# Earlier token preparation and wider spacing of the weight conversion in a fused attention and MoE kernel

## The chip, the cores and the metric

The kernel runs on one core of one Trainium2 chip. The metric is the device time of one execution in microseconds (us). PE is the matrix engine, DVE, ACT and POOL are the vector, scalar and GpSimd engines, SP is the queue that issues most DMA transfers.

## The reference, cut to what matters

```python
# attention: q, k, v are (4, 8, 576, 64)
q_rot, k_rot = rotate(q), rotate(k)              # RoPE: x1*cos - x2*sin, x1*sin + x2*cos
scores = np.matmul(q_rot, k_rot.transpose(0, 1, 3, 2)) / np.sqrt(D)
attn = np.exp(scores - scores.max(-1, keepdims=True))
attn = attn / (attn.sum(-1, keepdims=True) + 1e-09)
x = np.matmul(attn, v)                           # -> (2304, 512)
# MoE 1: w_in (512, 2048), w_out (2048, 512)
h = np.maximum(x @ w_in, 0.0);  x = h * h @ w_out
# MoE 2: the same sizes, alpha (2048)
h = x @ w_in;  out = (np.maximum(h, 0) + alpha * np.minimum(h, 0)) @ w_out
```

The MoE weights come as float64 and are turned into pairs of float32 numbers on the chip.

## The kernel before

**Attention.** 32 heads are worked in 16 pairs (0 to 15) of 9 steps, 144 steps in all. A step forms scores (L205), takes their maximum (DVE, L208) and exponential (ACT, L209), and for a block of four steps ago transposes (PE, L226), splits into high and low parts (ACT L214 `pth`, DVE L215 `ptl`) and multiplies by v (L271). v is split by POOL (L131, L132, `vs`). Keys and queries of the next pair are rotated and transposed into `nat` (ACT L147, DVE L148), and SP copies them into `kH`, `qT` and `kL` ("the stack" of a pair, L173, twelve DMAs).

**First MoE stage.** Two blocks of 384 tokens ("first blocks") go through layer 1 while its weights are converted: 64 units of 12 matmuls, 32 for `w_in` (L535 to L537, result `ph`) and 32 for `w_out` (L553, result `py`, or `ph` for the second block). A unit is one block by one of 16 weight chunks. After these come all other token blocks and layer 2, from kept weights.

**A weight chunk** is loaded by SP (L379, 512 KB of float64) and goes through C = three DVE operations (L388, L389, L394), "grow" on ACT (L398), S = three DVE operations (L403, L404 and the join's L410), and the join's copy on ACT (L409). Each stage has a distance in units from the chunk's place; a chunk comes every 1.8 units. Beside this, `w_out` units need `gh` (ACT, L490) and `gl` (DVE, L491), and `w_in` units need `g` (ACT L575, then ACT L581 or POOL L583).

**The tokens x of the first blocks** come in eight parts ("x chunks"): SP loads them (L502, L504), POOL adds and scales (L512, L513, `xt`), ACT takes the high part (L520, `xs`) and POOL the low part (L526).

**Order.** The MoE is a generator that attention advances once a step for the last steps; inside a step each job is emitted by its distance, and every engine runs its instructions in the order in which they were emitted. The buffers of q, k, v and RoPE ("front") close when the generator starts, and the MoE takes their place.

Of the kernel before, what the change touches and what calls it, by code (L numbers as in the profile page):

```python
# [10 lines left out]
F32 = mybir.dt.float32  # L11
F32R = mybir.dt.float32r
U32 = mybir.dt.uint32
# [6 lines left out]
B, H, S, D = 4, 8, 576, 64  # L20
HALF = D // 2
NT, DM, DFF = B * S, H * D, 2048
P = 128
# [6 lines left out]
NR = 10  # L30
# [4 lines left out]
KQB, STB, PTB = 2, 2, 3  # L35
RB = 1
ROPE_AT, TURN_AT = 5, (0, 1, 2)
AHEAD_X = 14
OP0, OPD0, OP1, OPD1 = 2, 2, 0, 2
OP, OPD, OV = 0, 2, 3  # L40

# [1 line left out]
def attention(tc, q, k, v, ident, ident_d, rope_d, xd, rd, follow):  # L43
# [10 lines left out]
    with ExitStack() as at:  # L54
        pool = lambda name, bufs, **kw: at.enter_context(tc.tile_pool(name=name, bufs=bufs, **kw))
        front = at.enter_context(ExitStack())
        fpool = lambda name, bufs, **kw: front.enter_context(tc.tile_pool(name=name, bufs=bufs, side="right", **kw))
# [3 lines left out]
        st_ = pool("asums", 1)  # L61
        lds = [fpool("ald0", 1)]
        cp = fpool("acst", 1)
        rp = fpool("arope", 1)
        lds.append(fpool("ald1", 1))
        scored = at.enter_context(ExitStack())
        nat = scored.enter_context(tc.tile_pool(name="anat", bufs=1))
        kq = scored.enter_context(tc.tile_pool(name="akq", bufs=KQB))
        scored.enter_context(tc.manual_schedule(engines={mybir.EngineType.PE}))
# [14 lines left out]
        rot = {}  # L84
# [23 lines left out]
        def rope(n, nm, c0=0, c1=NR, E=G):  # L108
            w = c1 - c0
            x = raw[n // 2 % 2, nm][:, 2 * (n % 2):2 * (n % 2) + 2]  # L110
            x = x.rearrange("p h r (t d) -> p (h r) t d", t=2)[:, c0:c1]
            c, ns, s = ((tabq if nm == "q" else tab)[:, c0:c1, i] for i in range(3))
            if (n, nm) not in rot:
                rot[n, nm] = rp.tile([P, 5, 2, D], F32, name=f"rot{nm}", bufs=2)
            r = rot[n, nm][:, :, c0 // 5:c1 // 5].rearrange("p r j d -> p j r d")
            t1 = rp.tile([P, NR, 2, HALF], F32, name="t1", bufs=RB)[:, 0:w]
            t2 = rp.tile([P, NR, 2, HALF], F32, name="t2", bufs=1)[:, 0:w]
            E.tensor_tensor(out=t1, in0=x, in1=c.unsqueeze(2).to_broadcast([P, w, 2, HALF]), op=ALU.mult)
            E.tensor_tensor(out=t2[:, :, 0], in0=x[:, :, 1], in1=ns, op=ALU.mult)
            E.tensor_tensor(out=t2[:, :, 1], in0=x[:, :, 0], in1=s, op=ALU.mult)  # L120
            t1, t2 = (t.rearrange("p (j r) t d -> p j r (t d)", r=5) for t in (t1, t2))
            E.tensor_tensor(out=r, in0=t1, in1=t2, op=ALU.add)
# [159 lines left out]
        steps = [(n, i, j) for n in range(len(pairs)) for i, j in order]  # L282
        per = len(order)
        load(0, "k", 0, 1, nc.gpsimd)
        table(0)
        load(0, "k", 1, 2, nc.gpsimd)
# [24 lines left out]
        for s in range(len(steps) + LAG + OP + 3 * OPD + 8):  # L311
            if s < len(steps):
                n, i, j = steps[s]
# [12 lines left out]
            if LAG <= s and s - LAG < len(steps):  # L326
                n, i, j = steps[s - LAG]
# [15 lines left out]
            for f, a in later.pop(s, []):  # L343
                f(*a)
            if s == len(steps) - AHEAD_X:
                front.close()
            if s == len(steps) - 1:
                scored.close()
            if s >= len(steps) - AHEAD_X:
                follow()  # L350


NB, W = 6, 384
FIRST = 2
STEPS_AHEAD, EARLY = 8, 2
HELD0, OUT0, OUTX, AHEAD = 4, 7, 2, 2
CONV0, EVERY0, EVERY1, EVERY2 = -8, 1.8, 1.8, 2.9


class Weights:  # L360
# [6 lines left out]

    def __init__(self, tc, mats, pbias, place, done):
        self.nc, self.mats, self.pbias, self.place, self.done = tc.nc, mats, pbias, place, done
        self.parts = {}  # L370

        self.stages = (((-3, self.load), (0, self.convert), (0, self.mask), (1, self.grow), (2, self.sign), (2, self.join)),
                       ((-3, self.load), (0, self.convert), (1, self.mask), (2, self.grow), (3, self.sign), (4, self.join)))

    def load(self, st, *j):
        layer, z, i = j
        src, c = (self.mats[layer][0][:, i * P:(i + 1) * P], KC) if z == 0 else (self.mats[layer][1][i * P:(i + 1) * P, :], 1)
        w64 = st.tile([P, 512, 2], U32, name="w64", bufs=4)
        self.nc.sync.dma_start(out=w64.rearrange("p (c n) t -> p c (n t)", c=c),  # L379
                               in_=src.bitcast(U32).rearrange("(c p) n -> p c n", p=P))  # L380
        self.parts[j] = w64

    def convert(self, st, *j):
        V = self.nc.vector
        w64 = self.parts[j]
        lo, hi = w64[:, :, 0], w64[:, :, 1]
        m = st.tile([P, 512], U32, name="m", bufs=2)
        V.tensor_scalar(m, hi, 0x1FF, None, ALU.bitwise_and)  # L388
        V.scalar_tensor_tensor(out=m.bitcast(F32), in0=lo, scalar=2.0 ** -32, in1=m, op0=ALU.mult, op1=ALU.add)  # L389
        self.parts[j] = lo, hi, m  # L390
# [24 lines left out]
def moe(tc, xd, rd, mats, pbias, dram, al, out):  # L415
# [11 lines left out]
    with ExitStack() as mo:  # L427
        pool = lambda name, bufs, **kw: mo.enter_context(tc.tile_pool(name=name, bufs=bufs, **kw))
# [4 lines left out]
        Xw = [Xf[:, 1024 * k:1024 * k + 1024].rearrange("p (y n) -> p y n", y=2) for k in range(6)]  # L433

        XT = pool("xt", 1, side="right").tile([P, 2, 3, W], F32, name="xt")
        st = pool("st", 1, side="right")
        x2 = dram.tile([P, KC, NT], F32, name="x2")
        XW = FIRST * W

# [4 lines left out]
        at_unit = {u: t for t, u in enumerate(units)}  # L444
# [18 lines left out]
        weights = Weights(tc, mats, pbias, place, done_with)  # L463
# [137 lines left out]
        NF = at_unit[0, FIRST, 0, 0]  # L601

        jobs = {}

        def job(at, stages, *j):
            for d, stage in stages:
                jobs.setdefault(max(int(at // 1) + d, -STEPS_AHEAD - 1), []).append((-d, stage, j))

        conv = [[(d, lambda *j, f=f: f(st, *j)) for d, f in stages] for stages in weights.stages]
        for k in range(2 * FC):  # L610
            if k < HELD0:
                job(CONV0 + 2 * k, conv[0][1:], 0, 0, k)
                continue
            at = EARLY + EVERY0 * (k - HELD0)
            if k >= FC + OUT0 + OUTX:
                at = max(at, at_unit[0, FIRST - 1, 1, FC // 2 - 1] - 2 + EVERY1 * (k - FC - OUT0 - OUTX))
            job(at, conv[0], 0, k // FC, k % FC)
        for k in range(2 * FC):
            job(NF + EVERY2 * k, conv[1], 1, k // FC, k % FC)
        for c in range(KC):  # L620
            for layer in range(2):
                for b in range(0 if layer else FIRST, NB):
                    before = (layer, b - 1) if b else (layer - 1, NB - 1)
                    job((NF - 16 if before == (0, FIRST - 1) else at_unit[before + (1, 0)]) + 4 * c + 1,
                        ((-2, load_x), (0, join_x), (1, high_x), (2, low_x)), layer, b, c)


        for e in range(AHEAD_X):
            for k in range(FIRST * KC):
                for d, stage in ((0, load_x), (2, join_x), (2, high_x), (2, low_x)):  # L630
                    if 3 * k // 2 + d == e:
                        stage(0, *divmod(k, KC))
            if e % 3 == 1 and e // 3 < HELD0:
                weights.load(st, 0, 0, e // 3)
            yield
        late["held0"] = pool("held0", HELD0, side="right")
        ps_h = pool("ps_h", 4, side="right", space=PSUM)
        mo.enter_context(tc.manual_schedule(engines={ET.PE, ET.DVE, ET.Activation, ET.Pool}))

        unfinished = []  # L640
        for t in range(-STEPS_AHEAD - 1, NU + 1):
# [18 lines left out]
            if 0 <= t < NU:  # L660
                layer, b, z, i = units[t]
# [6 lines left out]
@with_exitstack  # L668
def fused_kernel(ctx: ExitStack, tc: tile.TileContext, q, k, v, w_in1, w_out1, w_in2, w_out2, alpha, ident_d, rope_d, out):
    nc = tc.nc  # L670
    const = ctx.enter_context(tc.tile_pool(name="const", bufs=1))
    dram = ctx.enter_context(tc.tile_pool(name="dram", bufs=1, space=DRAM))
    ident = const.tile([P, P], F32, name="ident")
    al = const.tile([P, FC], F32, name="al")
    pbias = const.tile([P, 1], F32, name="pbias")
    nc.gpsimd.memset(pbias, -float(896 * 2 ** 23))
    xd = dram.tile([2, P, KC, NT], F32, name="x1")
    rd = dram.tile([KC, 2, NT], F32, name="r1")
    rest = moe(tc, xd, rd, ((w_in1, w_out1), (w_in2, w_out2)), pbias, dram, al, out)
# [43 lines left out]
```

## Time and profile before

| | |
|---|---|
| median of three runs | 1176.19 us (1176.02 to 1178.01) |
| the profiled execution | 1178.72 us |
| its span in the profile | 1176.9 us |
| PE busy | 1097.0 us, 93% of the span |
| DVE busy | 693.4 us, 59% |
| ACT busy | 567.4 us, 48% |
| POOL busy | 396.3 us, 34% |

The span starts with the first instruction of the profile and ends with the last. Overlapping instructions of one engine are counted once in its busy time. The share of an engine is a mean over stages of very different kinds; the stage of the 64 units lies between 342.3 and 506.0 us, attention ahead of it.

### The profile page before, as it was taken

What the parts mean: (1) busy time and instruction counts of PE and PEld (TensorE: products, weight loads), DVE (VectorE), ACT (ScalarE), POOL (GpSimd) and SP (SyncE); (2) the same over time, 40 slices, a digit from 0 to 9 for tenths busy, and PEclk for the clock granted to TensorE, in tenths of its full rate; (3) what the DMA queues carried; (4) which work ended last, traced back from release to release, by engine and by line L of the source; (5) the groups of instructions that cost most, each with busy time, mean ns of one, the idle gap of its engine ahead of it and who ended that gap; (6) DMA issues with size and microseconds to landing.
All of it is one profiled execution on the core that took longest, in us unless ns stands there. A gap on an engine that the chain in (4) does not pass through costs nothing.

```text
span 1176.9 us, 17871 instructions
## 1 busy us (share of the span) xinstructions
PE 1097.0 (93%) x6480; PEld 1041.5 (88%) x6480; DVE 693.4 (59%) x1211; ACT 567.4 (48%) x1228; POOL 396.3 (34%) x372
## 2 busy tenths in 40 slices
PE   2899999999869979899999999999999999999997
PEld 1789898898859869799999999999998989899996
DVE  3788888888778887857868690223232332323231
ACT  1687878878746544455554643323232222323222
POOL 7957566561442230113131221023140504122140
PEclk9899999999888979999999999999999999999999
DMA  8766676454773432455857648840102001010101
GB/s 241 174 180 174 179 203 180 131 152 121 195 222 116 125 109 84 146 177 184 256 172 247 211 155 256 265 158 7 48 1 54 1 27 27 14 41 7 35 1 27
DMA packets 97495, 150.18 MB, mean 128 GB/s; under 512 B 21760, under 2 KB 66432, under 8 KB 97408
## 3 DMA queue, kind: packets, MB, share of 16 engines
q1 hardware_dynamic: 91792, 138.85, 41.3%
q10 hardware_dynamic: 5360, 10.07, 2.3%
q8 instruction: 51, 0.84, 0.3%
q14 instruction: 36, 0.29, 0.1%
q0 software_dynamic: 256, 0.13, 0.0%
HBM read 84.98 MB, written 35.73 MB: 103 GB/s over the span
## 4 chain that ended last, share of the span: by engine, by line
PE 68%; DVE 16%; ACT 4%; DMA 3%; issue 3%; POOL 3%; SPq 1%; ACTq 0%; POOLq 0%
PE py L553 24%; PE ph L535 9%; PE ph L536 9%; PE ph L537 9%; PE acc L271 5%; PE sc L205 5%; PE ps L226 3%; DVE w L403 3%; DVE m L389 2%; DVE w L404 2%; DVE m L388 2%; DVE gl L491 2%; PE ph L553 2%; DVE w L410 1%; DVE nat L148 1%
## 5 line engine op out<-in xcount | busy, mean ns | idle before, releaser
L535 PE MATMUL ph<-xs,w 128*128 128x384 f32 x768 | 258.6, 337 | 5.6 <-ACT g L575 5.6
L536 PE MATMUL ph<-xs,w 128*128 128x384 f32 x768 | 257.8, 336 | 0.0
L537 PE MATMUL ph<-xs,w 128*128 128x384 f32 x768 | 257.7, 336 | 0.0
L491 DVE TENSOR_TENSOR gl<-g,gh 128x384 fp32r<-128x384 f32 x192 | 109.5, 571 | 193.5 <-ACT gh L490 193.4
L579 POOL TENSOR_TENSOR g<-g,xt 128x384 f32<-128x384 f32 x96 | 101.8, 1060 | 295.6 <-DVE xt L578 295.6
L575 ACT ACTIVATE g<-ph 128x384 f32<-128x384 f32 x192 | 93.7, 488 | 194.7 <-PE ph L537 187.2
L490 ACT ACTIVATE gh<-g 128x384 fp32r<-128x384 f32 x192 | 99.8, 521 | 149.5 <-PE py L553 126.6
L553 PE MATMUL py<-w,gh 128*128 128x512 f32 x504 | 155.3, 389 | 0.0
L535 PEld LDWEIGHTS ph<-xs,w 128*128 128x128 f32 x768 | 145.0, 189 | 7.6 <-ACT g L575 7.3
L553 PE MATMUL py<-gh,w 128*128 128x384 f32 x560 | 148.0, 339 | 2.8 <-ACT gh L490 2.8
L536 PEld LDWEIGHTS ph<-xs,w 128*128 128x128 f32 x768 | 145.0, 189 | 0.2
L537 PEld LDWEIGHTS ph<-xs,w 128*128 128x128 f32 x768 | 145.0, 189 | 0.0
L578 DVE TENSOR_SCALAR xt<-ph,al 128x384 f32<-128x384 f32 x96 | 59.3, 617 | 138.8 <-ACT g L575 131.7
L208 DVE TENSOR_REDUCE nm<-sc 128x1 f32<-128x576 f32 x144 | 105.8, 751 | 22.6 <-PE sc L205 21.2
L583 POOL TENSOR_TENSOR g<-g 128x384 f32<-128x384 f32 x48 | 46.2, 962 | 214.7 <-ACT g L575 206.2
L209 ACT ACTIVATE p<-sc,nm 128x576 f32<-128x576 f32 x144 | 106.4, 740 | 24.3 <-DVE nm L208 17.6
L215 DVE TENSOR_TENSOR ptl<-ps,pth 128x512 fp32r<-128x512 f32 (+1 forms) x160 | 99.8, 631 | 21.7 <-ACT pth L214 19.2
L553 PEld LDWEIGHTS py<-w,gh 128*128 128x128 f32 x504 | 94.5, 188 | 19.4
L214 ACT ACTIVATE pth<-ps 128x512 fp32r<-128x512 f32 (+1 forms) x160 | 86.9, 554 | 40.5 <-PE ps L226 39.4
L553 PEld LDWEIGHTS py<-gh,w 128*128 128x128 f32 x560 | 103.3, 191 | 3.5 <-ACT gh L490 3.5
L553 PE MATMUL py<-gl,w 128*128 128x384 f32 x280 | 95.8, 342 | 2.8 <-DVE gl L491 2.6
L553 PE MATMUL py<-w,gl 128*128 128x512 f32 x252 | 98.2, 390 | 0.0
(118 smaller groups left out, 1987.9 us busy)
## 6 DMA issues: line engine op xcount, KB each, us to landing
w<-in_moe_w_in_dram SPq DMA_DIRECT2D x32, 512.0 KB
w<-in_moe_w_out_dram SPq DMA_DIRECT2D x32, 512.0 KB
wk<-xs SPq DMA_DIRECT2D x32, 512.0 KB
w<-wk SPq DMA_DIRECT2D x30, 512.0 KB
xt<-x SPq DMA_DIRECT2D x72, 192.0 KB
kH<-nat SPq DMA_DIRECT2D x64, 144.0 KB
qT<-nat SPq DMA_DIRECT2D x64, 144.0 KB
kL<-nat SPq DMA_DIRECT2D x64, 144.0 KB
```

The costliest lines, as they stand in the source:

```text
L208: V.tensor_reduce(out=nm, in_=sc[:, :, 0:SH], axis=AX.XY, op=ALU.max, negate=True)
L209: A.activation(out=Pt[n, i][:, j * S:(j + 1) * S].rearrange("p (a b) -> p a b", a=2), in_=sc[:, :, 0:SH], func=AF.Exp, bias=nm, accum_out= ...
L214: A.activation(out=sl(hi), in_=src, func=AF.Copy)
L215: V.tensor_tensor(out=sl(lo), in0=src, in1=sl(hi).bitcast(F32), op=ALU.subtract)
L490: A.activation(out=hi, in_=g, func=AF.Copy)
L491: V.tensor_tensor(out=lo, in0=g, in1=hi.bitcast(F32), op=ALU.subtract)
L535: T.matmul(ph[:, :W], lhsT=wh[:, cs], rhs=xh, start=(c == 0), stop=False)
L536: T.matmul(ph[:, :W], lhsT=wh[:, cs], rhs=xl, start=False, stop=False)
L537: T.matmul(ph[:, :W], lhsT=wl[:, cs], rhs=xh, start=False, stop=(c == KC - 1))
L553: T.matmul(acc, lhsT=x, rhs=y, start=(s0 and k == 0), stop=(s1 and k == 2))
L575: A.activation(out=g, in_=ph, func=AF.Relu)
L579: G.tensor_tensor(out=g, in0=g, in1=mn, op=ALU.add)
```

## The change

The rows of the changed kernel carry line numbers that are one higher inside attention and four higher in the MoE (L208 becomes L209, L403 becomes L407).

- The generator starts 21 attention steps ahead of the end of the scores instead of 14; the x chunks are spaced 9/4 steps apart instead of 3/2. For this the front buffers close earlier, and the rotated keys and the second `vraw` buffer move to a pool that lives as long as the scores.
- The stages of the first four weight chunks get a table of times (`FIRST_AT`, counted in units from the first one). The first chunk's C, grow and sign stand beside attention. Chunks 0 and 1 are loaded early, 2 and 3 after the scores' buffers close, and the staging tiles are split over two pools.
- In layer 1, grow moves one unit later and sign and join move one unit later.
- The x jobs of later blocks start one unit earlier, and their ACT and DVE parts keep their place.

```diff
-AHEAD_X = 14
+AHEAD_X = 21
...
-        rp = fpool("arope", 1)
-        lds.append(fpool("ald1", 1))
+        rt = fpool("arope", 1)
         scored = at.enter_context(ExitStack())
+        lds.append(scored.enter_context(tc.tile_pool(name="ald1", bufs=1)))
+        rp = scored.enter_context(tc.tile_pool(name="arot", bufs=2))
...
-CONV0, EVERY0, EVERY1, EVERY2 = -8, 1.8, 1.8, 2.9
+
+FIRST_AT = (-15, -15, -14, -12, -9), (-9, -9, -9, -7, -7), (-5, -5, -5, -4, -4), (-3, -3, -3, -2, -2)
+EVERY0, EVERY1, EVERY2 = 1.8, 1.8, 2.9
...
-        self.stages = (((-3, self.load), (0, self.convert), (0, self.mask), (1, self.grow), (2, self.sign), (2, self.join)),
+        self.stages = (((-3, self.load), (0, self.convert), (0, self.mask), (2, self.grow), (3, self.sign), (3, self.join)),
...
-        w64 = st.tile([P, 512, 2], U32, name="w64", bufs=4)
+        n = next(self.count)
+        w64 = st[n // 2 % 2].tile([P, 512, 2], U32, name="w64", bufs=2)
...
-        m = st.tile([P, 512], U32, name="m", bufs=2)
+        m = st[n % 2].tile([P, 512], U32, name="m")
...
-                job(CONV0 + 2 * k, conv[0][1:], 0, 0, k)
+                for d, (_, stage) in zip(FIRST_AT[k], conv[0][1:]):
+                    if d < -STEPS_AHEAD - 1:
+                        before.setdefault(AHEAD_X + STEPS_AHEAD + 1 + d, []).append((stage, (0, 0, k)))
+                    else:
+                        jobs.setdefault(d, []).append((0, stage, (0, 0, k)))
...
-                    job((NF - 16 if before == (0, FIRST - 1) else at_unit[before + (1, 0)]) + 4 * c + 1,
-                        ((-2, load_x), (0, join_x), (1, high_x), (2, low_x)), layer, b, c)
+                    job((NF - 16 if prior == (0, FIRST - 1) else at_unit[prior + (1, 0)]) + 4 * c,
+                        ((-2, load_x), (0, join_x), (2, high_x), (3, low_x)), layer, b, c)
...
-                    if 3 * k // 2 + d == e:
+                    if 9 * k // 4 + d == e:
                         stage(0, *divmod(k, KC))
-            if e % 3 == 1 and e // 3 < HELD0:
-                weights.load(st, 0, 0, e // 3)
+            if e in (6, 9):
+                weights.load(st, 0, 0, e // 9)
+            for stage, j in before.get(e, []):
+                stage(*j)
             yield
+        st.append(pool("st1", 1, side="right"))
         late["held0"] = pool("held0", HELD0, side="right")
+        for k in range(2, HELD0):
+            weights.load(st, 0, 0, k)
```

DVE, at the start of the stage (chunks 5 and 6 of `w_in`). `m` is the mask tile and `w64` the float64 chunk, each with its number; before:

```order
L388 TENSOR_SCALAR m_4992<-w64_4925 128x512
L389 SCALAR_TENSOR_TENSOR m_4992<-w64_4925,m_4992 128x512
L394 TENSOR_SCALAR w64_4925<-w64_4925 128x512
L403 SCALAR_TENSOR_TENSOR w64_4925<-w64_4925 128x512
L404 TENSOR_SCALAR w64_4925<-w64_4925 128x512
L410 SCALAR_TENSOR_TENSOR w_5032<-m_4992,w64_4925 128x512
L388 TENSOR_SCALAR m_5035<-w64_4969 128x512
L389 SCALAR_TENSOR_TENSOR m_5035<-w64_4969,m_5035 128x512
L394 TENSOR_SCALAR w64_4969<-w64_4969 128x512
```

The same place in the changed kernel:

```order
L392 TENSOR_SCALAR m_4994<-w64_4932 128x512
L393 SCALAR_TENSOR_TENSOR m_4994<-w64_4932,m_4994 128x512
L398 TENSOR_SCALAR w64_4932<-w64_4932 128x512
L407 SCALAR_TENSOR_TENSOR w64_4870<-w64_4870 128x512
L408 TENSOR_SCALAR w64_4870<-w64_4870 128x512
L414 SCALAR_TENSOR_TENSOR w_5015<-m_4950,w64_4870 128x512
L392 TENSOR_SCALAR m_5037<-w64_4970 128x512
L393 SCALAR_TENSOR_TENSOR m_5037<-w64_4970,m_5037 128x512
L398 TENSOR_SCALAR w64_4970<-w64_4970 128x512
L407 SCALAR_TENSOR_TENSOR w64_4932<-w64_4932 128x512
```

C of a chunk was followed at once by S of the same chunk; now C of the next chunk stands between them.

POOL, in the last two pairs of attention (`vs` is v of pairs 13 to 15, `xt` and `xs` the x chunks); before:

```order
L131 CAST vs<-vraw_111 128x10x64
L132 TENSOR_TENSOR vs<-vraw_111,vs 128x10x64
L131 CAST vs<-vraw_114 128x10x64
L132 TENSOR_TENSOR vs<-vraw_114,vs 128x10x64
L131 CAST vs<-vraw_114 128x10x64
L132 TENSOR_TENSOR vs<-vraw_114,vs 128x10x64
L512 TENSOR_TENSOR xt<-xt 128x384
L513 TENSOR_TENSOR xt<-xt 128x384
L526 TENSOR_TENSOR xs<-xt,xs 128x384
```

The same place in the changed kernel:

```order
L132 CAST vs<-vraw_114 128x10x64
L133 TENSOR_TENSOR vs<-vraw_114,vs 128x10x64
L516 TENSOR_TENSOR xt<-xt 128x384
L517 TENSOR_TENSOR xt<-xt 128x384
L530 TENSOR_TENSOR xs<-xt,xs 128x384
L132 CAST vs<-vraw_117 128x10x64
L133 TENSOR_TENSOR vs<-vraw_117,vs 128x10x64
L516 TENSOR_TENSOR xt<-xt 128x384
L517 TENSOR_TENSOR xt<-xt 128x384
L530 TENSOR_TENSOR xs<-xt,xs 128x384
```

One x chunk now stands ahead of v of pair 14; in the rows that follow, three more stand ahead of v of pair 15, and four behind it. All eight stood behind pair 15's before.

SP, around the stack of pair 15 (`xt` the loads of x chunks); before:

```order
L173 DMA kH<-nat 64x576 x4
L173 DMA qT_119<-nat 64x576 x4
L173 DMA kL<-nat 64x576 x4
L502 DMA xt<-x_64 64x2x384
L173 DMA kH<-nat 64x576 x4
L173 DMA qT_120<-nat 64x576 x4
L173 DMA kL<-nat 64x576 x4
L504 DMA xt<-r_65 64x384
```

The same place in the changed kernel:

```order
L174 DMA kL<-nat 64x576 x4
L508 DMA xt<-r_65 64x384
L506 DMA xt<-x_64 64x2x384
L508 DMA xt<-r_65 64x384
L506 DMA xt<-x_64 64x2x384
L508 DMA xt<-r_65 64x384
L506 DMA xt<-x_64 64x2x384
L508 DMA xt<-r_65 64x384 x3
L506 DMA xt<-x_64 64x2x384 x2
L174 DMA kH<-nat 64x576 x4
```

The rest of x chunk 1 and the whole loads of x chunks 2 and 3 stand between the stacks of pairs 14 and 15, where one load stood before.

## Rows read from the trace of the kernel before

**Rows 1.** Windows: from:to, length, busy and (count) by engine, PE clock, DMA share, GB/s.

```profile
250.00:300.00 50.00, 46.24 (x367) 44.42 (x366) 43.58 (x79) 40.66 (x104) 11.52 (x10) 1.00 0.53 139
303.00:324.00 21.00, 17.51 (x119) 16.69 (x118) 13.57 (x25) 13.99 (x36) 14.18 (x14) 0.84 0.68 191
342.30:506.00 163.70, 145.98 (x770) 140.37 (x769) 134.29 (x225) 81.47 (x151) 26.08 (x25) 0.94 0.41 126
506.00:1176.90 670.90, 663.80 (x3554) 627.80 (x3552) 288.58 (x499) 241.81 (x473) 160.68 (x152) 1.00 0.33 102
```

**Rows 2.** Chain of waits: start, us, what; one undisturbed unit of the stage.

```profile
445.27 2.08 PE py L553 x12
```

**Rows 3.** Timeline of PE: start, us, instruction, [idle before, releaser]; the stage's start.

```profile
342.30 0.34 PE L535 MATMUL ph<-xs,w 128*128 128x384 f32 x1
...
354.56 0.69 PE L535 MATMUL ph<-xs,w 128*128 128x384 f32 x1 [3.76 <-ACT g L575]
...
360.16 0.37 PE L537 MATMUL ph<-xs,w 128*128 128x384 f32 x1
```

**Rows 4.** Waits of PE, 342.3 to 506: us in total, times, longest.

```profile
PE ph L553 <- DVE gl L491: 7.3, 5, 4.0
PE ph L535 <- ACT g L575: 5.6, 5, 3.8
PE py L553 <- ACT gh L490: 2.8, 2, 2.4
PE py L553 <- DVE gl L491: 1.7, 2, 1.6
```

**Rows 5.** Waits of DVE, 342.3 to 506.

```profile
DVE gl L491 <- ACT gh L490: 12.2, 15, 1.5
DVE w L403 <- ACT w L398: 10.1, 15, 0.8
```

**Rows 6.** Timeline of DVE in the stage: a `w_in` chunk, then two `w_out` stretches.

```profile
346.04 0.42 DVE L388 TENSOR_SCALAR m<-w 128x512 uint32<-128x512 uint32 x1
...
348.48 0.69 DVE L403 SCALAR_TENSOR_TENSOR w<-w 128x512 uint32<-128x512 uint32 x1 [0.83 <-ACT w L398]
...
350.28 0.42 DVE L388 TENSOR_SCALAR m<-w 128x512 uint32<-128x512 uint32 x1
...
428.78 1.32 DVE L403 SCALAR_TENSOR_TENSOR w<-w 128x512 uint32<-128x512 uint32 x1
...
435.59 0.55 DVE L491 TENSOR_TENSOR gl<-g,gh 128x384 fp32r<-128x384 f32 x1
436.91 0.56 DVE L491 TENSOR_TENSOR gl<-g,gh 128x384 fp32r<-128x384 f32 x1 [0.77 <-ACT gh L490]
437.39 0.68 DVE L403 SCALAR_TENSOR_TENSOR w<-w 128x512 uint32<-128x512 uint32 x1
...
439.18 0.42 DVE L388 TENSOR_SCALAR m<-w 128x512 uint32<-128x512 uint32 x1
...
440.70 0.55 DVE L491 TENSOR_TENSOR gl<-g,gh 128x384 fp32r<-128x384 f32 x1
```

**Rows 7.** Timelines of POOL, ACT and PE around the first x chunks, and the tail.

```profile
306.49 0.99 POOL L513 TENSOR_TENSOR xt<-xt 128x384 f32<-128x384 f32 x1
...
307.51 0.52 ACT L520 ACTIVATE xs<-xt 128x384 fp32r<-128x384 f32 x1 [1.94 <-POOL xt L513]
...
310.11 0.39 PE L244 MATMUL ps<-ident,p 128*64 128x128 f32 x1 [3.26 <-DVE ptl L215]
...
333.36 0.42 PE L244 MATMUL ps<-ident,p 128*64 128x128 f32 x1 [5.15 <-DVE pttl L215]
```

**Rows 8.** Timelines of POOL, SP and PE: v of pair 14, stack and scores of pair 15.

```profile
285.61 1.55 POOL L132 TENSOR_TENSOR vs<-vraw,vs 128x640 fp32r<-128x640 f32 x1
...
290.70 2.54 SPq L173 DMA_DIRECT2D kH<-nat  x4
...
300.49 0.51 PE L205 MATMUL sc<-kH,qT 128*128 128x288 f32 x2
```

More of the change, by code (lines that the diff above doesn't have):

```diff
@@ L113, in rope @@
             if (n, nm) not in rot:
-                rot[n, nm] = rp.tile([P, 5, 2, D], F32, name=f"rot{nm}", bufs=2)
+                rot[n, nm] = rp.tile([P, 5, 2, D], F32, name=f"rot{nm}")
             r = rot[n, nm][:, :, c0 // 5:c1 // 5].rearrange("p r j d -> p j r d")
-            t1 = rp.tile([P, NR, 2, HALF], F32, name="t1", bufs=RB)[:, 0:w]
-            t2 = rp.tile([P, NR, 2, HALF], F32, name="t2", bufs=1)[:, 0:w]
+            t1 = rt.tile([P, NR, 2, HALF], F32, name="t1", bufs=RB)[:, 0:w]
+            t2 = rt.tile([P, NR, 2, HALF], F32, name="t2", bufs=1)[:, 0:w]
             E.tensor_tensor(out=t1, in0=x, in1=c.unsqueeze(2).to_broadcast([P, w, 2, HALF]), op=ALU.mult)
@@ L369, in __init__ @@
         self.nc, self.mats, self.pbias, self.place, self.done = tc.nc, mats, pbias, place, done
-        self.parts = {}
-        self.stages = (((-3, self.load), (0, self.convert), (0, self.mask), (1, self.grow), (2, self.sign), (2, self.join)),
+        self.parts, self.count = {}, itertools.count()
+        self.stages = (((-3, self.load), (0, self.convert), (0, self.mask), (2, self.grow), (3, self.sign), (3, self.join)),
                        ((-3, self.load), (0, self.convert), (1, self.mask), (2, self.grow), (3, self.sign), (4, self.join)))
@@ L377, in load @@
         src, c = (self.mats[layer][0][:, i * P:(i + 1) * P], KC) if z == 0 else (self.mats[layer][1][i * P:(i + 1) * P, :], 1)
-        w64 = st.tile([P, 512, 2], U32, name="w64", bufs=4)
+        n = next(self.count)
+        w64 = st[n // 2 % 2].tile([P, 512, 2], U32, name="w64", bufs=2)
         self.nc.sync.dma_start(out=w64.rearrange("p (c n) t -> p c (n t)", c=c),
                                in_=src.bitcast(U32).rearrange("(c p) n -> p c n", p=P))
-        self.parts[j] = w64
+        self.parts[j] = n, w64
     def convert(self, st, *j):
         V = self.nc.vector
-        w64 = self.parts[j]
+        n, w64 = self.parts[j]
         lo, hi = w64[:, :, 0], w64[:, :, 1]
-        m = st.tile([P, 512], U32, name="m", bufs=2)
+        m = st[n % 2].tile([P, 512], U32, name="m")
         V.tensor_scalar(m, hi, 0x1FF, None, ALU.bitwise_and)
@@ L435, in moe @@
         XT = pool("xt", 1, side="right").tile([P, 2, 3, W], F32, name="xt")
-        st = pool("st", 1, side="right")
+        st = [pool("st0", 1, side="right")]
         x2 = dram.tile([P, KC, NT], F32, name="x2")
@@ L609, in moe @@
         conv = [[(d, lambda *j, f=f: f(st, *j)) for d, f in stages] for stages in weights.stages]
+        before = {}
         for k in range(2 * FC):
             if k < HELD0:
-                job(CONV0 + 2 * k, conv[0][1:], 0, 0, k)
+                for d, (_, stage) in zip(FIRST_AT[k], conv[0][1:]):
[3 more added lines that the diff above has]
+                        jobs.setdefault(d, []).append((0, stage, (0, 0, k)))
                 continue
@@ L622, in moe @@
                 for b in range(0 if layer else FIRST, NB):
-                    before = (layer, b - 1) if b else (layer - 1, NB - 1)
-                    job((NF - 16 if before == (0, FIRST - 1) else at_unit[before + (1, 0)]) + 4 * c + 1,
-                        ((-2, load_x), (0, join_x), (1, high_x), (2, low_x)), layer, b, c)
+                    prior = (layer, b - 1) if b else (layer - 1, NB - 1)
+                    job((NF - 16 if prior == (0, FIRST - 1) else at_unit[prior + (1, 0)]) + 4 * c,
+                        ((-2, load_x), (0, join_x), (2, high_x), (3, low_x)), layer, b, c)
         for e in range(AHEAD_X):
```

## The prediction

> **What bounds the kernel now.** I read the windows by stage first [rows 1]. From 506.00 to the end the matrix engine is busy 663.80 of 670.90 us at a granted clock of 1.00, and between 250 and 300 us, in steady attention, 46.24 of 50. What is left to win lies between: 303 to 324 us (busy 17.51 of 21, clock 0.84) and the stage of 64 units, 342.30 to 506.00 us, busy 145.98 of 163.70 at clock 0.94. The chain of waits gives the price of an undisturbed unit there, 12 matmuls in 2.08 us [rows 2]; 64 such units are 133.1 us, so the stage loses 163.7 - 133.1 = 30.6 us. The waits of the matrix engine name 7.3 + 5.6 + 2.8 + 1.7 = 17.4 us of it [rows 4]; the other 13.2 are mostly matmuls at the lower clock level after such a wait. The timeline shows one: after a wait of 3.76 us the matmuls from 354.56 to 360.16, 17 intervals, take 5.60 us [rows 3], where 17/12 of a unit at full clock would be 2.95 [rows 2]; 2.65 us lost behind a wait of 3.76.
>
> Behind those waits stand the vector and scalar engines with the conversion. A `w_in` chunk goes round in 350.28 - 346.04 = 4.24 us, 0.83 of it waiting for the scalar engine's grow [rows 6]; the matrix engine uses a chunk up in two units, 4.16 us. The wait for grow is 10.1 us over the stage in 15 records [rows 5]. The vector engine is busy 134.29 us of the stage [rows 1], as much as the matrix engine's ideal 133.1: it is the second bound, close below.
>
> **The wider spacing.** With C of the next chunk ahead of S, three vector operations, 1.5 us together, lie between grow's input and its user: C is 440.70 - 439.18 = 1.52 us, S 439.18 - 437.39 = 1.79 [rows 6], and grow's wait was 0.83. So the 0.83 goes, and a `w_in` chunk costs 3.41 us, below 4.16: in the first 32 units the vector engine no longer falls behind. The wait at the fifth unit also goes. Between the last operations of attention and the first `g`, the old vector order holds S of chunk 0 and C and S of chunks 1 to 3, three and a half cycles; the new one holds chunks 2 and 3, two cycles. One and a half cycles of 4.24 are 6.4 us, more than the wait of 3.76 [rows 3]. With it go the 2.65 us at the lower level.
>
> In the `w_out` half the vector engine also makes `gl`, 0.48 us each (436.91 to 437.39 [rows 6]). By the table of times, twelve units in its first part hold 12 `gl`, about 7 S and 5 C: 5.8 + 12.5 + 7.6 = 25.9 us. Two more terms: where POOL runs x joins beside it, S and C took 435.59 - 428.78 = 6.81 instead of 440.70 - 437.39 = 3.31 us [rows 6], 3.5 more, and two waits for `gh` of 0.77 [rows 6], 1.5. In all 30.9 against 12 x 2.08 = 25.0 for the matrix engine, 5.9 over. It starts two units ahead, 2 x 2.08 - 0.48 = 3.7 us of cover, so about 2.2 us of wait are left. A second part of fourteen units (14 `gl`, 7 C, 7 S, and 2.6 us of waits and POOL's presence) comes to 6.7 + 10.6 + 12.5 + 2.6 = 32.4 against 29.1, 3.3 over: hidden by the cover if that has been won back, up to 3.3 if not; I take half, 1.8. Waits in the stage then sum to 4.0, and as 17.4 us of waits brought 13.2 of other loss, 0.76 for each, another 3.0. The stage: 133.1 + 4.0 + 3.0 = 140.1, a gain of 23.6 us. The bounds: all 30.6 (no wait left), and 10.1 (only grow's wait goes and the vector engine sets the pace).
>
> **The earlier x chunks and the first weight chunk.** Now beside attention: for each of four x chunks two POOL joins and a subtraction of about 0.99 and a copy of 0.52 on the scalar engine [rows 7]; C of chunk 0 and the first two operations of its S, about 2.6 us of the vector engine [rows 6], and grow. In steady attention POOL is busy 11.52 of 50 us, the scalar engine 40.66, the vector engine 43.58 [rows 1], so the work fits on average into about 40 us. But it stands in a fixed order: a copy that waits for POOL holds back the exponentials and splits queued behind it, and the matrix engine waits for those. The one case in the trace is the first x chunk: the copy waited 1.94 us for POOL, then the matrix engine 3.26 us for `ptl` [rows 7], and the window around it has clock 0.84, 21 x 0.16 = 3.4 us at most lost to it [rows 1]. So such a place costs up to 3.26 + 3.4 = 6.7 us. With the slack of the averages it costs nothing. I see two tight places. One is SP's queue: the last loads of x chunk 3 wait for x chunk 1's subtraction, and that follows v of pair 14, which ends at 285.61 + 1.55 = 287.16 [rows 8]. Two joins, the copy and the subtraction, 1.98 + 0.52 + 0.99, give 290.65, and two loads at 2.54/4 us of issuing each 291.9: the stack of pair 15, issued from 290.70, comes some 1.2 us later, and its first score stands at 300.49 [rows 8]. Its own slack no row gives; cost 0 to 1.2. The other is the vector engine with chunk 0. I take one half of a place for all, 3.3 us, with bounds 0 and 6.7. The place at 310.11 itself stays, since the fifth x chunk still follows v of pair 15.
>
> What the trace shows of vector and POOL work side by side: S and C took 6.81 us instead of 3.31 where POOL ran x joins [rows 6]. The Trainium skill, "SBUF — State Buffer", section "SBUF: two separate sides", says that these two engines share a port pair as a lock held for a whole instruction, so that the other blocks fully. The stretch agrees. By that rule the five operations of chunk 0 beside attention, each held for one POOL operation of about 1 us, would cost 5 us instead of 3.3, an estimate; the sum would then be 1.7 higher.
>
> **The tail of attention, 324 to 342.** Four x chunks less, but join of chunk 0 and C and S of chunk 1 more, about 0.7 (some two fifths of S) + 3.3 - 1.5 = 2.5 us of the vector engine ahead of its last splits. The matrix engine waits 5.15 us there for `pttl` [rows 7]; the vector work can fall into that or lengthen it. Zero, bounds -2.5 and 2.5.
>
> **Loads, pools and later x jobs.** The first two weight loads wait less than the old ones, being issued far earlier; a chunk's staging tile is held for 3 + 3 units of 1.8 per chunk, 3.3 of 4 tiles, so loads are not held back. After 506.00 the new order of the x jobs moves only work of engines that are not waited for; 7.1 us of that window are all that could move [rows 1]. Zero for both.
>
> **Sum.** 1176.9 - 23.6 + 3.3 = 1156.6 us of span. The profiled execution took 1178.72 us, 1.8 above its span, so 1158.4; the median 1176.19 is 2.5 below that execution, and so the forecast is 1156 us.
>
> **Rivals.**
> - The vector engine sets the stage's pace. For: it is busy 134.29 us there, beside POOL's joins its operations double, and the waits for `gh`, 12.2 us [rows 5], are not touched. Against: it leaves idle time in the first 32 units that it could use. Then only grow's 10.1 us go: 1176.9 - 10.1 + 3.3 - 0.7 = 1169 us. Chance 0.16.
> - The matrix engine waits nowhere in the stage, and attention absorbs everything: 1176.9 - 30.6 - 0.7 = 1146 us. For: average idle time in attention; against: the second half's balance above. Chance 0.14, of which most falls a little short of 1146.
> - Slower: each of the four x chunks beside attention does what the first one does now, a scalar copy that waits for POOL, splits behind it, and a lower clock after: 4 x 6.7 = 26.8 us. It decides from the fourth such place (23.6 / 6.7 = 3.5). 1176.9 - 23.6 + 26.8 - 0.7 = 1179 us. For: rows 7; against: ahead of x chunks 1 to 3 POOL has been idle long enough and their loads are early. Chance 0.04.
> - The change doesn't do what it says: chunks come no earlier, since loads of chunks 2 and 3, now issued only when the scores' buffers close, make the first conversions late, and the two-and-two staging keeps them so. The stage stays at 163.7: 1176.9 + 3.3 - 0.7 = 1179.5 us. Chance 0.02.
>
> **How the numbers follow.** The forecast's own case has 0.62, with 1150 to 1164 from its bounds. A further 0.02 goes to a near balance, the second case with two bad places in attention. The range 1146 to 1168 leaves out about half of the first rival, the slow cases and a little below. A difference of 0.2%, about 2.4 us, is what a measurement of this kernel can tell from no change. Faster: 0.62 + 0.16 + 0.14 = 0.92; same 0.02; slower 0.04 + 0.02 = 0.06.
>
> **What would show it.** In the profile after: L407 with almost no wait for L402; no wait at the fifth unit; the stage within 137 to 145 us; the remaining waits of L557 for `gl` in the `w_out` half; the first of them beside POOL's x joins. In attention a total longer by at most 7 us, with the loss at x chunks 1 to 3 or the first scores of pair 15. The forecast is wrong if the stage gains under 16 us, or if attention with its tail, up to the first unit, moves by more than 7.

## The result, and the profile after

The changed kernel takes 1165.39 us (1165.12 to 1166.19, 4 runs) against 1176.9 for the one before (4 runs): a ratio of 0.9903 with an interval of 0.9886 to 0.992. It is 11.5 us faster, where 20 were forecast; the range holds it, the likeliest case's own range of 1150 to 1164 does not. The two profiled executions lie a little further apart, 1176.9 and 1163.8 us of span, and the rows below are theirs.

The windows after, cut at the same pieces of work (the first unit now stands at 349.21, the first matmul after the 64 units at 494.51 us):

```profile
250.00:300.00 50.00, 43.27 (x324) 40.80 (x325) 42.12 (x78) 36.75 (x94) 21.80 (x20) 0.97 0.67 179
303.00:324.00 21.00, 18.01 (x131) 17.34 (x130) 15.12 (x27) 15.08 (x38) 10.35 (x11) 0.92 0.56 162
349.20:494.50 145.30, 137.63 (x770) 135.71 (x769) 129.17 (x215) 79.66 (x148) 25.51 (x24) 0.98 0.42 127
494.50:1163.80 669.30, 663.16 (x3554) 627.92 (x3552) 286.95 (x499) 242.62 (x473) 160.18 (x152) 1.00 0.33 103
```

Against [rows 1] the stage went from 163.7 to 145.3 us, 18.4 less; the rest from 670.9 to 669.3; and steady attention, 46.24 us of matrix work in 50 before, has 43.27. Up to the first unit the kernel is 6.9 us later, and as this execution ran 0.7 us ahead at 250 us, attention lost 7.6.

The waits of the matrix engine in the stage after, answering to [rows 4], and of the vector engine, to [rows 5]:

```profile
PE ph L557 <- DVE gl L495: 5.6, 4, 2.5
PE py L557 <- DVE gl L495: 1.9, 1, 1.9
PE ph L557 <- ACT gh L494: 0.2, 1, 0.2
```

```profile
DVE gl L495 <- ACT gh L494: 7.3, 6, 1.6
DVE g L599 <- PE py L557: 2.4, 2, 1.9
DVE w L407 <- ACT w L402: 1.5, 2, 0.8
```

The wait for grow fell from 10.1 to 1.5 us and no unit waits for `g` any more. What is left, 7.7 us, is for `gl` and `gh` in the `w_out` half, most of it for `gl`. The vector engine there, and POOL beside it:

```profile
418.31 2.46 DVE L495 TENSOR_TENSOR gl<-g,gh 128x384 fp32r<-128x384 f32 x2
420.69 1.50 DVE L407 SCALAR_TENSOR_TENSOR w<-w 128x512 uint32<-128x512 uint32 x1
...
423.39 1.38 DVE L414 SCALAR_TENSOR_TENSOR w<-m,w 128x512 fp32r<-128x512 f32 x1
...
426.33 0.55 DVE L495 TENSOR_TENSOR gl<-g,gh 128x384 fp32r<-128x384 f32 x1
```

```profile
417.99 1.08 POOL L587 TENSOR_TENSOR g<-g 128x384 f32<-128x384 f32 x1 [0.61 <-ACT g L579]
419.03 1.32 POOL L516 TENSOR_TENSOR xt<-xt 128x384 f32<-128x384 f32 x1
...
423.15 1.07 POOL L517 TENSOR_TENSOR xt<-xt 128x384 f32<-128x384 f32 x1
```

```profile
426.94 0.69 PE L557 MATMUL ph<-gl,w 128*128 128x384 f32 x1 [2.47 <-DVE gl L495]
```

From 418.31 to 426.33 stand two `gl`, an S and a C: 8.0 us, where the undisturbed rows give 2 x 0.48 + 3.31 = 4.3 [rows 6]. The `gl` that ended at 426.9 is the one for which the matrix engine waited 2.47 us. The scalar engine is not what holds the stretch up: its longest waits in the stage are for the vector engine, the 4.3 us one at 422 us, and its wait rows name no POOL operation.

```profile
ACT w L413 <- DVE w L407: 39.3, 24, 4.3
```

The first `gl` of the `w_out` half is done 1.4 us ahead of its unit (413.80 + 0.56 against 415.78):

```profile
413.80 0.56 DVE L495 TENSOR_TENSOR gl<-g,gh 128x384 fp32r<-128x384 f32 x1
...
415.78 0.33 PE L557 MATMUL py<-gh,w 128*128 128x384 f32 x1
```

In attention the first loss is at the first weight chunk. The timelines of four engines around it, where the first column is the start and the last bracket the idle time before:

```profile
266.67 1.55 POOL L133 TENSOR_TENSOR vs<-vraw,vs 128x640 fp32r<-128x640 f32 x1
267.08 1.42 DVE L392 TENSOR_SCALAR m<-w 128x512 uint32<-128x512 uint32 x1 [0.47 <-DMA w<-in_moe_w_in_dram]
...
268.54 0.68 DVE L393 SCALAR_TENSOR_TENSOR m<-w,m 128x512 f32<-128x512 uint32 x1
269.15 0.75 DVE L209 TENSOR_REDUCE nm<-sc 128x1 f32<-128x576 f32 x1
269.81 0.68 DVE L149 TENSOR_TENSOR nat<-ps,nat 128x512 fp32r<-128x512 f32 x1
269.93 0.74 ACT L210 ACTIVATE p<-sc,nm 128x576 f32<-128x576 f32 x1 [1.61 <-DVE nm L209]
...
270.64 0.63 PE L227 MATMUL ps<-ident,p 128*128 128x128 f32 x4 [2.47 <-DVE nat L149]
```

The mask waited 0.47 us for its load, took 1.42 instead of 0.42 [rows 6] and ended at 268.50, just behind POOL's subtraction (268.22). The maximum and `nat` queued behind it, and the matrix engine waited 2.47 us. The Trainium skill, "SBUF — State Buffer", section "SBUF: two separate sides", says that a GpSimd operation and a vector operation that runs in a 2-port mode or has two SBUF inputs take a shared port pair as a lock, and that the other one is fully blocked for the whole instruction. The trace agrees, with 1.42 us against 0.42; no run shows in which mode this mask, which has one input, ran.

The second kind of loss, at x chunk 3:

```profile
299.07 1.01 POOL L517 TENSOR_TENSOR xt<-xt 128x384 f32<-128x384 f32 x1
...
300.11 0.52 ACT L524 ACTIVATE xs<-xt 128x384 fp32r<-128x384 f32 x1 [2.05 <-DMA kH<-nat]
300.66 0.60 ACT L215 ACTIVATE pth<-ps 128x512 fp32r<-128x512 f32 x1
...
301.15 0.73 ACT L210 ACTIVATE p<-sc,nm 128x576 f32<-128x576 f32 x1
...
302.03 0.52 PE L206 MATMUL sc<-kH,qT 128*128 128x288 f32 x2 [1.37 <-ACT p L210]
```

The copy starts when POOL's join ends (299.07 + 1.01 = 300.08; the transfer that the bracket names is not its input), and an exponential behind it makes the scores wait 1.37 us.

### The profile page after: what moved, and what is told of

Same layout as the page of the kernel before. It is cut to its first block, busy times and chain, and to the rows that moved or that the text cites. A ratio compares the mean times of both kernels' runs of the same rounds, so it can differ in the third digit from the quotient of the medians.

```text
span 1163.8 us, 17882 instructions
## 1 busy us (share of the span) xinstructions
PE 1089.9 (94%) x6480; PEld 1037.0 (89%) x6480; DVE 688.3 (59%) x1211; ACT 568.2 (49%) x1228; POOL 394.6 (34%) x372
## 4 chain that ended last, share of the span: by engine, by line
PE 72%; DVE 14%; DMA 4%; POOL 4%; issue 3%; ACT 2%; SPq 1%; POOLq 0%; DVEq 0%; ACTq 0%
PE py L557 28%; PE ph L540 10%; PE ph L541 10%; PE ph L539 10%; PE acc L272 5%; PE sc L206 4%; PE ps L227 3%; PE ph L557 2%; DVE m L393 2%; DVE w L407 2%; DMA kraw<-in_k_dram 2%; DVE w L408 1%; DVE w L414 1%; DVE nat L149 1%; DVE ptl L216 1%
## 5 line engine op out<-in xcount | busy, mean ns | idle before, releaser
L209 DVE TENSOR_REDUCE nm<-sc 128x1 f32<-128x576 f32 x144 | 105.7, 751 | 22.0 <-PE sc L206 20.6
L216 DVE TENSOR_TENSOR ptl<-ps,pth 128x512 fp32r<-128x512 f32 (+1 forms) x160 | 99.8, 631 | 22.8 <-ACT pth L215 20.7
L227 PE MATMUL ps<-ident,p 128*128 128x128 f32 x576 | 89.1, 278 | 12.9 <-DVE nat L149 9.0
```

The costliest lines, as they stand in the source:

```text
L209: V.tensor_reduce(out=nm, in_=sc[:, :, 0:SH], axis=AX.XY, op=ALU.max, negate=True)
L216: V.tensor_tensor(out=sl(lo), in0=src, in1=sl(hi).bitcast(F32), op=ALU.subtract)
L227: T.transpose(u[:, c * P:(c + 1) * P], p[:, (S + 64) * j + c * P:(S + 64) * j + (c + 1) * P], ident)
```

## The experiments

All kernels give the matrix engine the same work in the same order, so the start of one and the same matmul can be compared between profiles. The table says how many us a kernel gained (-) or lost (+) against the kernel before, between five fixed matmuls that start at 266.30, 273.97, 300.35, 342.30 and 506.03 us there. A column is read from one profiled execution of each kernel; the last column is the median of its runs, with the ratio and its interval.

| kernel | first weight chunk, to 273.97 | x chunks, to 300.35 | rest of attention, to 342.30 | 64 units, to 506.03 | median us; ratio |
|---|---|---|---|---|---|
| the change | +3.5 | +3.6 | +0.4 | -18.4 | 1165.39; 0.9903 (0.9886 to 0.992) |
| e1 | 0.0 | 0.0 | +0.4 | -15.6 | 1162.65; 0.9873 (0.986 to 0.9887) |
| e2 | +2.7 | +4.0 | -0.2 | -7.2 | 1177.69; 1.0002 (0.9992 to 1.0011) |
| e3 | +3.5 | +1.2 | -3.8 | -19.8 | 1160.12; 0.9851 (0.9832 to 0.9871) |
| e4 | +3.2 | +3.7 | +0.4 | -25.8 | 1158.22; 0.9834 (0.9817 to 0.985) |
| e5 | 0.0 | +3.6 | +0.6 | -18.5 | 1161.53; 0.9863 (0.9844 to 0.9882) |
| e6 | +2.4 | +1.1 | -0.7 | -19.6 | 1160.47; 0.9851 (0.9834 to 0.9868) |
| e7 | 0.0 | +1.3 | +3.3 | -19.5 | 1161.43; 0.9859 (0.984 to 0.9877) |
| e8 | 0.0 | 0.0 | -5.3 | -13.1 | 1160.23; 0.985 (0.9832 to 0.9867) |
| e9 | +2.8 | +4.0 | -1.3 | -25.3 | 1158.03; 0.9831 (0.9817 to 0.9845) |
| e10 | 0.0 | 0.0 | -4.3 | -20.0 | 1151.65; 0.9775 (0.9762 to 0.9789) |
| e11 | +3.2 | +1.2 | +0.4 | -26.1 | 1156.61; 0.9821 (0.9807 to 0.9834) |

How far single executions scatter can be read from kernels whose attention holds the same instructions in the same order. Those that keep the early weight chunk beside v of pair 13 have +2.4 to +3.5 in the first column; e3, e6 and e11 have -3.8, -0.7 and +0.4 in the third. Smaller differences in those two columns show nothing.

**e1, the distances alone, on the kernel before.**

```diff
-(1, self.grow), (2, self.sign), (2, self.join)),
+(2, self.grow), (3, self.sign), (3, self.join)),
```

> The kernel before with only the distances of layer 1's conversion changed (grow 1 to 2, sign and join 2 to 3). Theory A (the stage's gain comes from the spacing; attention's loss of the changed kernel comes from the early x chunks and weight chunk): attention ends at 342 as before, no wait of L403 for L398, but the wait of about 4 us at the fifth unit stays with some 2.6 us of matmuls at the lower clock; 1164 to 1167 us. Theory B (without the early weight chunk the first units stay late and the spacing gives little): at most 6 us less than before, 1170 us or more.

Measured 1162.65 us, a little below what theory A gave: this one edit is worth no less than the whole change (0.9873 against 0.9903, intervals that just touch). The stage gains 15.6 us alone and attention loses nothing before the tail. The vector engine's wait for grow is 0.2 us in the stage. The wait at the fifth unit is 0.9 us, not 4: the chunks ahead of the first `g` now follow each other in 350.31 - 346.86 = 3.45 us and not in 4.24.

```profile
346.86 0.69 DVE L403 SCALAR_TENSOR_TENSOR w<-w 128x512 uint32<-128x512 uint32 x1
...
350.31 0.69 DVE L403 SCALAR_TENSOR_TENSOR w<-w 128x512 uint32<-128x512 uint32 x1
```

```profile
PE ph L535 <- ACT g L575: 0.9, 1, 0.9
```

**e2, the early chunks alone.** The changed kernel with the old distances, in layer 1's conversion and in the later x jobs.

```diff
-(2, self.grow), (3, self.sign), (3, self.join)),
+(1, self.grow), (2, self.sign), (2, self.join)),
```

> The changed kernel with the old distances (grow 1, sign and join 2, x jobs as before), so only the early x chunks and weight chunks. Theory A: attention 7 us longer as in the changed kernel, the wait at the fifth unit gone (6 us), all other waits of the stage as before: 1175 to 1180 us, no gain. Theory B (the early start is what pays): 1171 us or less.

1177.69 us, no gain: attention loses 6.5 and the stage gains 7.2. The wait at the fifth unit is gone, which with the slower matmuls behind it was 3.76 + 2.65 us [rows 3]. So the early token and weight work, half of the change, brings nothing by itself. The two parts do not add up in the stage either, 15.6 + 7.2 = 22.8 against 18.4: each removes most of the wait at the fifth unit.

**e3, xs on POOL.**

```diff
-            A.activation(out=xh, in_=xin[layer, b, c][0][:, 0], func=AF.Copy)
+            if first(layer, b):
+                G.tensor_copy(out=xh, in_=xin[layer, b, c][0][:, 0])
+            else:
+                A.activation(out=xh, in_=xin[layer, b, c][0][:, 0], func=AF.Copy)
```

> The changed kernel with the high part of the first blocks' x chunks taken by POOL (a copy) instead of ACT, so that no ACT instruction waits for POOL's x joins. Theory A (ACT's copies that wait for POOL hold back the exponentials behind them): the losses of attention at x chunks 1 to 3 (1.7 and 1.65 us) and a part of those at chunks 4 and 5 go, 3 to 5 us: 1160 to 1162.5 us. Theory B (POOL and DVE hold each other up, and the scalar copy does not matter): four to eight more POOL operations beside DVE, 1165 to 1168 us.

1160.12 us: theory A. The loss at the x chunks falls from 3.6 to 1.2 us, and it is as small in e6, e7 and e11, which have the same edit; the 1.2 that stay were not followed up. The rest of attention gains 3.8 here, but not in e6 and e11. At the place shown above the exponential no longer stands behind a copy, and the same scores stand without a wait:

```profile
299.90 0.74 ACT L210 ACTIVATE p<-sc,nm 128x576 f32<-128x576 f32 x1
...
300.78 0.53 PE L206 MATMUL sc<-kH,qT 128*128 128x288 f32 x2
```

**e4, without the joins of the third block.**

```diff
-            if layer == 0:
+            if layer == 0 and b != FIRST:
                 G.tensor_tensor(out=xr[:, 0], in0=xr[:, 0], in1=xr[:, 1], op=ALU.add)
```

> The changed kernel without the two POOL joins of x for the third token block of layer 1 (its x stays unsummed and unscaled), the operations that ran at 419 to 424 and 474 to 487 us. Theory A (beside POOL's joins DVE's conversions take twice as long, and this makes the waits for gl): the 1.3 and 2.5 us waits at 419 and 427 us and the 1.2 and 1.9 us ones at 477 and 481 us go with half of the lower clock behind them, 5 to 8 us less: 1157 to 1160.5 us. Theory B (DVE has too much to do there whatever POOL does): at most 2 us less, 1163.5 us or more.

1158.22 us, 7.2 below the change, all of it in the stage (-25.8 against -18.4): theory A. Eight POOL operations cost 7.4 us of the stage. The first `gl` of the `w_out` half is as early as in the change; what goes are the slow operations behind it.

**e5, a late first weight chunk.** A 128x1 copy from x chunk 3 into the mask tile holds the conversion back to 300 us.

```diff
+        if j == (0, 0, 0):
+            V.tensor_copy(out=m[:, 0:1].bitcast(F32), in_=self.gate.bitcast(F32))
         V.tensor_scalar(m, hi, 0x1FF, None, ALU.bitwise_and)
...
+        weights.gate = X[:, 1, 3, 0:1]
```

> The changed kernel, whose first weight chunk's conversion on DVE waits for the copy of x chunk 3 (a 128x1 copy from it into the mask tile), so that it no longer stands beside v of pair 13 on POOL. Theory A (the 3.5 us lost at 267 us come from the first mask operation, which took 1.42 us instead of 0.42 beside that POOL copy after waiting for its load): attention is 2.5 to 3.5 us shorter, 1161.5 to 1163 us. Theory B (the conversion costs DVE as much wherever it stands, or collides with x chunks there): 1164.5 to 1167 us.

1161.53 us, theory A: the 3.5 us at 267 us are gone and nothing of them comes back. The run takes away two things at once, the mask's 0.47 us wait for its load and the 1.0 us by which POOL lengthened it, and does not tell them apart. With no POOL operation in the way the same mask takes 0.43 us:

```profile
300.15 0.43 DVE L394 TENSOR_SCALAR m<-w 128x512 uint32<-128x512 uint32 x1
```

**e6, the joins in the first half.** On e3, the third block's first two x chunks loaded and joined at units 10 to 16.

```diff
...
+                    if prior == (0, FIRST - 1) and c < 2:
+                        job(12 + 4 * c, ((-2, load_x), (0, join_x)), layer, b, c)
+                        job(at, ((2, high_x), (3, low_x)), layer, b, c)
+                        continue
...
```

> The kernel of e3 (xs on POOL), with the load and the POOL joins of the third block's first two x chunks issued at units 10 to 16 instead of straight behind the last square of the first half, the whole computation kept. Theory A (the joins hurt only where DVE is the bound): the waits for gl at units 33 to 35 go, 5 to 7 us less than e3: 1153 to 1155.5 us. Theory B (the time that they take from DVE comes back wherever they stand): 1158.5 to 1161 us.

1160.47 us: theory A fell. The stage is as in e3 (-19.6 against -19.8). The vector operations beside the joins are as slow in the first half as in the second:

```profile
371.60 1.38 DVE L414 SCALAR_TENSOR_TENSOR w<-m,w 128x512 fp32r<-128x512 f32 x1
373.02 1.12 DVE L392 TENSOR_SCALAR m<-w 128x512 uint32<-128x512 uint32 x1
```

So the vector engine has no slack in the first half that such work could use. That gave a new theory: it works through the stage almost without a pause, and what POOL takes from it anywhere is paid at the end. e9 and e10 test it.

**e7, e6 with the late first chunk of e5.**

> The kernel of e6 with the late first chunk of e5. Theory A (the three losses are apart and add up): e6 less 2 to 3.5 us, 1150 to 1153 us. Theory B (attention gives the 3.5 us back later anyway, as e3 shows where the loss of 3.5 us at 267 shrinks to 0.9 by the first unit): the same as e6 within 1 us.

1161.43 us, like e6, as theory B said, but not for its reason. The loss at 267 us is gone, and the rest of attention is 4.0 us worse than in e6 (+3.3 against -0.7). Most of that stands at one place, and the copy that holds the conversion back makes it: x chunk 3 is later here than in e5, the copy waits 1.89 us for POOL's subtraction and with it every vector operation behind it, the mask then takes 1.01 us, and the matrix engine waits 3.61 us for a `ptl`; before the same matmul it waited 1.05 us in e6.

```profile
308.99 0.15 DVE L393 COPY m<-xs 128x1 f32<-128x1 f32 x1 [1.89 <-POOL xs L536]
309.18 1.01 DVE L394 TENSOR_SCALAR m<-w 128x512 uint32<-128x512 uint32 x1
...
311.60 0.39 PE L245 MATMUL ps<-ident,p 128*64 128x128 f32 x1 [3.61 <-DVE ptl L216]
```

So this run does not test whether the two losses add up; that stays open.

**e8, the distances and xs on POOL, without the early chunks.** The edits of e1 and e3 on the kernel before.

> The kernel of e1 (the kernel before with the new distances alone) with the x chunks' high part on POOL. Theory A (ACT's copies that wait for POOL make the loss at 306 to 316 us of before): attention is 2 to 4 us shorter than in e1, 1158.5 to 1160.5 us, as good as e3, and the early x chunks and weight chunk of the change then buy nothing. Theory B (the early start is needed once ACT is free): 1162 us or more.

1160.23 us, as e3: theory A, and the early x chunks and weight chunk buy nothing. Attention is 5.3 us shorter than before, 4.5 of it between 300 and 319 us, so that the loss around 310 us of [rows 7] was the copy on ACT. The stage starts so early that it waits more at its own beginning (-13.1).

**e9, the squares on ACT, on the change.**

```diff
-                elif i % 2 == 0:
+                elif i % 2 == 0 or first(layer, b):
                     A.activation(out=g, in_=g, func=AF.Square)
```

> The changed kernel with all squares of the first blocks on ACT (16 of 32 ran on POOL). Theory A (DVE sets the stage's pace: from 349 to 430 us it has next to no idle time, and each POOL operation beside it holds it up by some 0.6 us): DVE's work of the first half gets up to 8 us shorter, the waits for gl at 419 and 427 us go or shrink, 4 to 7 us less than the changed kernel, 1158.5 to 1161.5 us. Theory B (ACT, with 8 us more and its copies and grow in one order with the squares, takes DVE's place): within 1.5 us of it, 1164 us or more.

1158.03 us, 7.4 below the change, as theory A said. From about the first unit to 430 us, first the change, then this kernel, where POOL does nothing:

```profile
349.20:430.00 80.80, 76.76 (x433) 75.87 (x432) 76.07 (x120) 50.17 (x93) 21.04 (x20) 0.98 0.41 126
```

```profile
347.00:430.00 83.00, 83.00 (x484) 83.00 (x484) 72.55 (x134) 62.11 (x116) 0.00 (x0) 1.00 0.43 134
```

The vector engine was busy 76.07 of 80.80 us (94%) for 120 operations, 0.63 us each; now 134 operations, not quite the same mix, take 72.55, 0.54 each, and the matrix engine has no idle time. ACT, with 62.11 of 83, has room for the squares.

The 7.4 us are not the squares' alone. With no square ahead of them in POOL's queue, the joins of the third block's first two x chunks ran ahead too: they stand between 331 and 344 us here, before the stage, and not at 419 to 424, and e4 shows that the joins alone are worth as much. What the squares cost by themselves can be read ahead of 412 us, where no such join stands in either kernel. One of the six vector operations of a chunk, first in the change from 349.2 to 412 us, then in e9 from 347 to 410 (count, busy us, mean ns, idle us before):

```profile
L393 DVE SCALAR_TENSOR_TENSOR m<-w,m 128x512 f32<-128x512 uint32 x16 | 13.3, 832 | 0.6
```

```profile
L393 DVE SCALAR_TENSOR_TENSOR m<-w,m 128x512 f32<-128x512 uint32 x17 | 11.8, 692 | 0.6
```

Three others shrink as well, and over 16 chunks the six means differ by 7.1 us, some 0.5 for each of the 14 squares in that window. So the first `gl` of the `w_out` half is done 3.3 us ahead of its unit (411.68 + 0.56 against 415.51), where it was 1.4 in the change:

```profile
411.68 0.56 DVE L495 TENSOR_TENSOR gl<-g,gh 128x384 fp32r<-128x384 f32 x1 [1.10 <-ACT gh L494]
...
415.51 0.33 PE L557 MATMUL py<-gh,w 128*128 128x384 f32 x1
```

**e10 and e11, the squares on ACT, on e8 and on e3.**

> The kernel of e8 (the kernel before with the new distances and xs on POOL) with all squares of the first blocks on ACT. Theory A: as in e9, 4 to 7 us less than e8, 1153.5 to 1156.5 us, the best so far. Theory B: like e8 within 1.5 us.

> The kernel of e3 (the changed kernel with xs on POOL) with all squares of the first blocks on ACT. If the early x chunks and weight chunk of the change are worth something once DVE has room, this is below e10 by more than 1 us, 1151 to 1154 us; if only the distances pay, it is like e10 or above it.

e10 takes 1151.65 us, 8.6 below e8 and the best of all; e11 1156.61. The stage is better with the early chunks (-26.1 against -20.0), but attention is 9.1 us worse (+4.8 in all against -4.3), of which some 4 lie in the column that scatters by as much. So with vector time freed, the early start costs more than it brings: 5.0 us in the medians. e10 also tells more of the squares than e9 does. In it the joins of the first two x chunks stand at 347 to 359 us, inside the first half as in e6; with the squares on POOL that move changed nothing (-19.6 in e6, -19.8 in e3), and with the squares gone as well the stage gains 6.9 (against e8). The two pairs start from different kernels, so this bears the theory out without proving it. e10 still waits 3.7 us for `gl`, and at its start 2.4 us for the first `g` and 1.2 for a join.

```profile
PE ph L538 <- ACT g L578: 2.4, 1, 2.4
PE py L556 <- DVE gl L491: 1.9, 1, 1.9
PE ph L556 <- DVE gl L491: 1.8, 2, 1.2
PE ph L540 <- DVE w L410: 1.2, 1, 1.2
```

## Why the prediction was right in direction and short in size

- **The wider spacing: right.** The wait for grow went (10.1 to 1.5 us), and e1 shows that this edit alone is worth 15.6 us of the stage. The first 32 units no longer wait, as forecast: from 349.2 to 412 us the matrix engine is busy all the time.
- **The wait at the fifth unit: right, for more than one reason.** It went in the change, and in e2 too, where the early chunks alone remove it. But e1, which keeps the late chunks, has only 0.9 us of it: the shorter chunk cycle would nearly do.
- **The `w_out` half: the mechanism right, the size too small.** Forecast were 4.0 us of waits and 3.0 of other loss; measured 7.7, and 145.3 - 133.1 - 7.7 = 4.5. (Half of 3.3 is 1.7 and not 1.8; that slip is worth 0.1 us.) The failed step is the cover of 3.7 us "two units ahead": the first `gl` was done 1.4 us ahead of its unit. With it fails the sentence in the first rival that the vector engine "leaves idle time in the first 32 units": in the change it is busy 94% of the time to 430 us, and comes to the `w_out` half with little to spare. POOL's x joins were priced rightly where they stand (3.5 us then, 3.7 now); its 16 squares in the first half were given no price, though vector operations are longer beside them too. With the squares gone the cover is 3.3 us (e9), close to the forecast's. e4 shows what the joins cost, 7.4 us of the stage, and e6 that moving them inside the stage changes nothing; how the 6.9 us of e9 divide between squares and joins no run shows. The rival of the vector engine's pace had the right cause with too high a price for it: 1169 us.
- **Attention: the failed term.** 3.3 us were forecast, with 6.7 as bound; 7.6 came. By the clock the first unit moved by 6.9 us; counted from 266 us, by 7.6, a little over the 7 that the forecast named as a sign of being wrong. The half place was two things. The first weight chunk costs 3.5 us by itself, where its first operation waited for its load and then stood beside v of pair 13 on POOL (e5). The forecast knew the doubling beside POOL, but had no place for it in the sum. The x chunks cost 3.6 us, and 2.4 of it go when the copy no longer waits on ACT for POOL (e3): the mechanism of the slower rival, with some 0.8 us for each of the three copies that waited and not 6.7. The other 1.2 us stay open.
- **SP's queue: the mechanism right, its price nothing.** The last loads of x chunk 3 went out at 293.76 us, as soon as x chunk 1's subtraction had ended (293.73), and the stack of pair 15 right behind them at 295.11, half a microsecond after the part of `nat` that `kH` reads was ready (294.62). The forecast gave this 0 to 1.2 us. The matrix engine's wait rows of that stretch name no transfer, so it cost nothing that they show.

```profile
292.73 1.00 POOL L530 TENSOR_TENSOR xs<-xt,xs 128x384 fp32r<-128x384 f32 x1 [0.64 <-ACT xs L524]
293.76 1.25 SPq L506 DMA_DIRECT2D xt<-x  x2
294.23 0.39 ACT L148 ACTIVATE nat<-ps 128x256 fp32r<-128x256 f32 x1
295.11 2.47 SPq L174 DMA_DIRECT2D kH<-nat  x4
```

- **The place at 310 us: right that it stays**, partly: the stretch from 300 to 319 us gained 1.5 us in the change, where e3 and e8 gain 4.2 and 4.5.
- **Tail and the later blocks:** +1.9 us between the matmuls at 319.32 and 342.30 in place of 0, and 1.6 us less after the 64 units: the first inside its bounds of 2.5, the second inside the 7.1 that could move.
- **The range of the likeliest case**, 1150 to 1164 us, is not worked out from its bounds, though the text says so: stage and attention at their ends give 1146 to 1173, and 1165.4 lies inside that.

## What to carry to other kernels

In these runs an operation's time on the vector engine is not a constant: ask for every long stretch of it what POOL runs beside it, and count that POOL work against the vector engine too. Here the matrix engine showed the waits of a stage whose pace a vector engine busy 94% of the time set; moving POOL's work earlier inside that stage gave nothing, and taking it out of the stage or to an engine with room did. Try each half of a change by itself: here one half did it all. When early work is put into a stage that is full, look at what stands behind each of its instructions in the same queue, above all behind a copy that waits for a third engine. And when an experiment takes instructions out of a queue, look at where those behind them went: in e9 they left the stage as well.

## What the runs showed that was not expected

A single 128x512 mask operation of 0.42 us, placed beside a POOL subtraction of 1.55 us, right behind a wait of 0.47 us for its load, moved the end of attention by 3.5 us (e5). And putting 16 squares on ACT, whose own price is 0.53 us each, shortened the vector engine's mean operation from 0.63 to 0.54 us (e9). Together with the joins that ran ahead by it, that was worth 7.4 us to a kernel whose matrix engine, busy 94% of the whole span, seemed the bound.
